# Storing the last gradient of wo in sixteen transfers of 15 down to 1 and 8 partitions in place of one

## The chip, the cores and the metric

The kernel runs on one core of a Trainium2 chip. The metric is the device time of one execution in microseconds (us). Each kernel is run several times, and the median is taken.

## The reference

The reference is one decode step of a transformer block with its backward pass. There is one token of 640 numbers, 32 heads of 128, and a cache of 8192 keys and values for each head. Everything is in bfloat16.

```
xn  = layernorm(x)
q   = xn @ wq                      # 640 x 4096, 32 heads of 128
p   = softmax(q . k_cache / sqrt(128))
att = (p . v_cache) @ wo           # wo is 4096 x 640
mlp = (silu(xn @ w1) * (xn @ w3)) @ w2
out = x + att + mlp
# the outputs: out, and the gradients of x, k_cache, v_cache, wq, wo, w1, w3, w2 for a given grad_out
```

The gradients of the caches are as large as the caches: 64 MB is read for each of K and V, and 64 MB is written for each gradient. The gradient of `wo` is an outer product: row n of it is `grad_out` times element n of the heads' outputs. It has 4096 rows of 640, and the kernel writes it in eight groups of four heads, 640 KB each.

## The kernel before, in words

The kernel begins with the feed-forward part (its products, its gradients of w1, w3 and w2), and then goes through the 32 heads. The loads of K and V for a head are 2 MB each and are issued by SyncE (SP). For each head VectorE multiplies K and V by the query and by the gradient row, TensorE sums the products, and VectorE and ScalarE form the two outer products that are the gradients of K and V, in tiles named `ot`. These are stored by GpSimd (POOL), 2 MB a tensor. In the last two heads (`TAIL = 2`) they are stored by SyncE instead, half a tensor (1 MB) at a time, at L456: eight such stores.

The order of instructions on every engine is written out by hand (`manual_schedule`). An engine works through its list in order. On SyncE, which has nothing but transfers, an issue that has to wait holds all issues behind it.

What comes after the loop is the tail. It finishes head 31, and then the following happens around the change:

- ScalarE forms the last quarter-group of the gradient of wq in `dwq_t` (L822) and issues its store of 640 KB itself (L824).
- VectorE forms the last group of the gradient of wo, in place in the tile `wo_g` (L826). SyncE stores it (L827), 128 partitions of four rows of 640, so 5120 bytes in a row of memory for each partition.
- VectorE and TensorE add up the remaining sums and finish the layernorm's backward pass (L832 to L853). Its result `dx_bf` is 1280 bytes, and SyncE stores it (L855).
- ScalarE stores the block's output `fin_bf`, five partitions of 256 bytes (L860).

Each transfer that SyncE or ScalarE issues counts up one of eight semaphores (`DMAHW0` to `DMAHW7`, numbers 100, 102, 103, 105, 106, 107, 109 and 110 in the trace) when its data has landed. The framework gives them out in turn, to both engines from one list, and a transfer that gets a semaphore waits at its issue until the transfer that had the semaphore before it has landed. In the kernel before, the eight stores of L456 have DMAHW4, 5, 6, 7, 0, 1, 2 and 3; then the store of `dwq_t` has DMAHW4, that of `fin_bf` DMAHW5, that of `wo_g` DMAHW6 and that of `dx_bf` DMAHW7. At the very end (L886) SyncE waits for all these semaphores, and the program ends.

Of the kernel before, what the change touches and what calls it, by code (L numbers as in the profile page):

```python
# [16 lines left out]
P = 128  # L17
# [4 lines left out]
def kernel(  # L22
# [22 lines left out]
    nc = tc.nc  # L45
# [23 lines left out]
    LANES = 16  # L69
# [26 lines left out]
    dwo_v = out_5.rearrange("(g p r) c -> g p r c", p=P, r=GH)  # L96
# [7 lines left out]
    with tc.manual_schedule(engines=ORDERED):  # L104
# [640 lines left out]
        for h in range(H - 1):  # L745
            n = new_head(h + 1) if h + 1 < H else None
            c = hs.pop(h)
            g, hh = divmod(h, GH)
# [50 lines left out]
        c = hs.pop(H - 1)  # L799
        g = c.g  # L800
# [23 lines left out]
        nc.scalar.dma_start(dwq_v[:, :, g * GH * DH:(g + 1) * GH * DH], dwq_t[:])  # L824
        for r in range(GH):
            nc.vector.tensor_scalar(c.G["wo"][:, r, :], g_bc_bf[:], on[:, r:r + 1], None, ALU.mult)  # L826
        nc.sync.dma_start(dwo_v[g], c.G["wo"][:])  # L827


        fin = consts.tile([P, NC], F32, name="fin")  # L830
# [3 lines left out]
        for ci in range(NC):  # L834
            k, c = divmod(ci * P, WIDE_COLS)
# [55 lines left out]
```

## Time and profile before

| what | value |
|---|---|
| median of 3 runs | 719.05 us (718.98 to 719.26) |
| the profiled execution, its time | 718.87 us |
| its span, first to last instruction | 717.1 us |
| PE, DVE, ACT busy | 78%, 88%, 68% of the span |
| moved | 303.32 MB, 423 GB/s in the mean |
| DMA issues of the tail | 1024 KB x8, 640 KB x2, 1.2 KB x2 |

The profiled execution lies 1.77 us above its span, and 0.18 us below the median of the runs. A page of the profile gives the busy time of each engine, the DMA share in forty slices, the chain of waits that ended last, groups of instructions with their mean duration, and the DMA issues with the time from issue to landing. "SPq" and "ACTq" are the sequencers of SyncE and ScalarE, which issue transfers. The chain of waits is followed back from the last instruction that computes; the stores that are still under way after it are not in it, and have to be read from the stretches of time after it and from the waits of SyncE.

### The profile page before, as it was taken

What the parts mean: (1) busy time and instruction counts of PE and PEld (TensorE: products, weight loads), DVE (VectorE), ACT (ScalarE), POOL (GpSimd) and SP (SyncE); (2) the same over time, 40 slices, a digit from 0 to 9 for tenths busy, and PEclk for the clock granted to TensorE, in tenths of its full rate; (3) what the DMA queues carried; (4) which work ended last, traced back from release to release, by engine and by line L of the source; (5) the groups of instructions that cost most, each with busy time, mean ns of one, the idle gap of its engine ahead of it and who ended that gap; (6) DMA issues with size and microseconds to landing.
All of it is one profiled execution on the core that took longest, in us unless ns stands there. A gap on an engine that the chain in (4) does not pass through costs nothing.

```text
span 717.1 us, 9854 instructions
## 1 busy us (share of the span) xinstructions
PE 557.1 (78%) x3516; PEld 272.4 (38%) x3516; DVE 630.6 (88%) x723; ACT 484.2 (68%) x1472; POOL 49.5 (7%) x91
## 2 busy tenths in 40 slices
PE   6878988878788777776887787488868789877772
PEld 4753443334333333333343344143434334333331
DVE  5789999999989895997899899499999889899982
ACT  1275778796769656694587867468677857777552
POOL 0010000000001110000000110000000000000100
PEclk9698999998989998997899989899999878999995
DMA  9999999999999999999999999999999999999997
GB/s 364 416 425 430 431 430 430 429 429 429 428 432 428 426 428 424 429 427 426 432 431 428 430 422 426 428 430 429 428 428 431 429 430 431 429 430 429 429 421 288
DMA packets 27039, 303.32 MB, mean 423 GB/s; under 512 B 3249, under 2 KB 3959, under 8 KB 9327
## 3 DMA queue, kind: packets, MB, share of 16 engines
q1 hardware_dynamic: 12832, 154.88, 50.9%
q0 software_dynamic: 10960, 137.72, 45.2%
q10 hardware_dynamic: 3198, 10.10, 3.5%
q8 instruction: 27, 0.44, 0.2%
q14 instruction: 22, 0.17, 0.1%
HBM read 151.34 MB, written 151.34 MB: 422 GB/s over the span
## 4 chain that ended last, share of the span: by engine, by line
DMA 45%; DVE 31%; PE 17%; ACT 3%; issue 2%; POOL 0%; ACTq 0%; DVEq 0%; POOLq 0%
DMA Kt<-in_A_k_cache_dram 28%; DVE T L425 15%; DMA out_dram<-ot 12%; DVE ot L451 10%; PE ob L500 4%; DMA lane_pad<-in_A_wq_dram 4%; PE psS L427 3%; PE psDP L427 3%; ACT ot L445 2%; DVE DP_sb L526 1%; DVE S_sb L472 1%; PE dh_ps L591 1%; PE dx_ps L626 1%; PE gate_ps L602 1%; PE ps_od L516 1%
## 5 line engine op out<-in xcount | busy, mean ns | idle before, releaser
L427 PE MATMUL psDP<-T,ident_bf 128*128 128x512 bf16 x512 | 157.0, 462 | 64.6 <-DVE T L425 64.6
L427 PEld LDWEIGHTS <-ident_bf 128*128 128x128 bf16 x1024 | 108.3, 109 | 212.6 <-issue 140.1
L445 ACT ACTIVATE ot<-qs_g,Uf 128x128 bf16<-128x128 bf16 x504 | 154.0, 394 | 45.1 <-DVE Uf L539 27.2
L425 DVE TENSOR_TENSOR T<-Kt,qs_g 128x4096 bf16<-128x4096 bf16 x64 | 146.4, 2287 | 20.0 <-DMA Kt<-in_A_k_cache_dram 18.8
L445 ACT ACTIVATE ot<-do_g,Pf 128x128 bf16<-128x128 bf16 x512 | 156.3, 389 | 6.2 <-DMA out_dram<-ot 5.2
L425 DVE TENSOR_TENSOR T<-Vt,do_g 128x4096 bf16<-128x4096 bf16 x64 | 146.0, 2282 | 3.9 <-DMA Vt<-in_A_v_cache_dram 3.9
L427 PE MATMUL psS<-T,ident_bf 128*128 128x512 bf16 x512 | 129.0, 397 | 17.7 <-DVE T L425 17.7
L451 DVE TENSOR_TENSOR ot<-qs_g,U 128x3072 bf16<-128x3072 bf16 (+2 forms) x64 | 112.6, 1760 | 11.9 <-DMA out_dram<-ot 11.8
L451 DVE TENSOR_TENSOR ot<-do_g,P 128x3072 bf16<-128x3072 bf16 (+2 forms) x64 | 112.3, 1755 | 6.3 <-DMA out_dram<-ot 5.2
L458 POOL DMA_DIRECT2D out_dram<-ot x60 | 32.2, 537 | 549.2 <-DVE Uf L539 303.6
L500 PE MATMUL ob<-Vt,P 128*4 128x512 bf16 x512 | 64.1, 394 | 0.0
L500 PE MATMUL ob<-Kt,U 128*4 128x512 bf16 x512 | 60.5, 379 | 1.4 <-DVE U L533 1.4
L494 ACT ACTIVATE Pf<-E,rZ 128x16 f32<-128x16 f32 (+1 forms) x32 | 9.8, 307 | 60.2 <-DVE rZ L489 60.2
L558 ACT ACTIVATE dq_diag<-ident_bf,odq 128x128 bf16<-128x128 bf16 x32 | 12.8, 401 | 47.8 <-DVE odq L554 47.8
L516 PEld LDWEIGHTS ps_od<-pick,wide 128*128 128x128 f32 x256 | 38.1, 213 | 7.8 <-issue 3.0
L516 PE MATMUL ps_od<-pick,wide 128*128 128x2 f32 x256 | 33.8, 254 | 0.5 <-ACT wide L508 0.5
L500 PEld LDWEIGHTS <-U 128*4 128x4 bf16 x512 | 19.8, 84 | 37.5 <-DVE U L533 6.6
L476 PE MATMUL sm<-ident_f,mrow 128*128 128x128 f32 x64 | 15.9, 331 | 22.3 <-DVE mrow L474 22.3
L500 PEld LDWEIGHTS <-P 128*4 128x4 bf16 x512 | 20.8, 86 | 25.8 <-issue 3.5
L508 ACT COPY wide<-ob 128x256 f32<-128x256 f32 x64 | 20.1, 363 | 12.7 <-PE ob L500 12.7
L472 DVE TENSOR_REDUCE S_sb<-psS 128x64 f32<-128x512 f32 x32 | 21.9, 685 | 5.6 <-PE psS L427 5.6
L317 ACT COPY woT<-ps_t 128x512 bf16<-128x512 bf16 x40 | 22.9, 577 | 4.2 <-PE ps_t L312 3.6
(174 smaller groups left out, 552.4 us busy)
## 6 DMA issues: line engine op xcount, KB each, us to landing
out_dram<-ot POOLq DMA_DIRECT2D x60, 2048.0 KB, 24.4
Kt<-in_A_k_cache_dram SPq DMA_DIRECT2D x32, 2048.0 KB, 26.6
Vt<-in_A_v_cache_dram SPq DMA_DIRECT2D x32, 2048.0 KB, 20.0
out_dram<-ot SPq DMA_DIRECT2D x8, 1024.0 KB, 12.7
out_dram<-wo_g ACTq DMA_DIRECT2D x6, 640.0 KB, 15.1
wo_g<-in_A_wo_dram ACTq DMA_DIRECT2D x6, 640.0 KB, 15.8
wq_two<-in_A_wq_dram SPq DMA_DIRECT2D x1, 2560.0 KB, 23.8
w1t<-in_B_w_dram SPq DMA_DIRECT2D x1, 2160.0 KB
```

What stands on the lines that cost most here:

```text
L317: nc.scalar.copy(woT[:], ps_t[:])
L425: nc.vector.tensor_tensor(T[:], src[:, :, ds_], vec[:, ds_].unsqueeze(1).to_broadcast([P, J, DHH]), ALU.mult)
L427: nc.tensor.matmul(ps[:], lhsT=ident_bf[:], rhs=T[:, :, RUN * i:RUN * (i + 1)], start=(half == 0 and i == 0), stop=(half == 1 and i == DHH ...
L445: nc.scalar.activation(st.ot[half][:, JH - n + j].rearrange("p a b -> p (a b)"), vec, ACTF.Copy, scale=wf[:, half, j:j + 1])
L451: nc.vector.tensor_tensor(st.ot[half][:, 0:n], vec.rearrange("p (a b) -> p a b", b=2).unsqueeze(1).to_broadcast([P, n, DH // 2, 2]), w2[:, ...
L458: nc.gpsimd.dma_start(dst.rearrange("p j d -> p (j d)"), st.rows[:])
L472: nc.vector.tensor_reduce(st.S[:], st.ps["S"][:], AX.X, ALU.add)
L476: nc.tensor.matmul(st.sm[:, 8:8 + P], lhsT=mrow[:].to_broadcast([P, P]), rhs=ident_f[:], start=True, stop=True, skip_group_check=True)
L500: nc.tensor.matmul(ob[c0:c0 + WIDE, :], lhsT=w2[:, WIDE * q:WIDE * (q + 1), 0], rhs=src[:, WIDE * q:WIDE * (q + 1), :].rearrange("p j d -> ...
L508: nc.scalar.copy(part[:], ob[:, i * (WIDE // 2) * DH:(i + 1) * (WIDE // 2) * DH])
L516: nc.tensor.matmul(st.od, lhsT=st.wide[i][:, b * DH:(b + 1) * DH], rhs=pick[:, r, :], start=(r == 0), stop=(r == WIDE - 1), skip_group_che ...
L558: nc.scalar.activation(dq_diag[:], ident_bf[:], ACTF.Copy, scale=odq[:, 1:2])
```

## The change

The one transfer of L827 becomes a loop of sixteen (L827 to L830 of the kernel after), all issued by SyncE, with the same bytes from the same tile. `LANES` is 16 and `P` is 128, so the counts of partitions are 15, 14, 13 and so on down to 1, which is 120 together, and then 8. Nothing else is changed; the later lines move down by three.

```diff
         for r in range(GH):
             nc.vector.tensor_scalar(c.G["wo"][:, r, :], g_bc_bf[:], on[:, r:r + 1], None, ALU.mult)
-        nc.sync.dma_start(dwo_v[g], c.G["wo"][:])
+        p0 = 0
+        for k in list(range(LANES - 1, 0, -1)) + [P - LANES * (LANES - 1) // 2]:
+            nc.sync.dma_start(dwo_v[g, p0:p0 + k], c.G["wo"][p0:p0 + k])
+            p0 += k
```

## The prediction

> **What bounds the kernel now.** I read the page first, then stretches of the tail, then SyncE's issues there, then its waits. The slices of the page:
>
> ```profile
> DMA  9999999999999999999999999999999999999997
> GB/s 364 416 425 430 431 430 430 429 429 429 428 432 428 426 428 424 429 427 426 432 431 428 430 422 426 428 430 429 428 428 431 429 430 431 429 430 429 429 421 288
> ```
>
> The DMA engines are full from first to last, so the kernel is bound by bytes until its last slice. There the stretches (busy time and count by engine, clock, DMA share, GB/s) show what is left:
>
> ```profile
> 700.00:708.00 8.00, 4.11 (x21) 3.08 (x21) 4.25 (x17) 3.13 (x6) 0.00 (x0) 0.61 1.01 419
> 708.00:712.00 4.00, 0.00 (x0) 0.00 (x0) 0.00 (x0) 0.00 (x0) 0.00 (x0) 0.50 0.76 285
> 712.00:714.00 2.00, 0.00 (x0) 0.00 (x0) 0.00 (x0) 0.00 (x0) 0.00 (x0) 0.50 0.38 137
> 714.00:715.00 1.00, 0.00 (x0) 0.00 (x0) 0.00 (x0) 0.00 (x0) 0.00 (x0) 0.50 0.10 34
> 715.00:717.10 2.10, 0.00 (x0) 0.00 (x0) 0.00 (x0) 0.00 (x0) 0.00 (x0) 0.50 0.00 1
> ```
>
> No engine computes after 708; stores alone set the end. The share falls in steps, so the sixteen DMA engines run dry one after the other, and at 0.10 one or two still work. Next the timeline of SyncE (start, length, issue), and the issues by tile (KB, us to landing):
>
> ```profile
> 702.11 0.41 SPq L827 DMA_DIRECT2D out_dram<-wo_g  x1
> 707.36 0.33 SPq L855 DMA_DIRECT2D out_dram<-dx_bf  x1
> ```
>
> ```profile
> out_dram<-ot SPq DMA_DIRECT2D x8, 1024.0 KB, 12.7
> out_dram<-wo_g SPq DMA_DIRECT2D x1, 640.0 KB, 13.4
> out_dram<-dwq_t ACTq DMA_DIRECT2D x1, 640.0 KB, 12.7
> out_dram<-dx_bf SPq DMA_DIRECT2D x1, 1.2 KB, 8.3
> ```
>
> Everything lands 8 to 13 us after its issue, because the queues are that long. Last, what SyncE waits for between 700 and 718:
>
> ```profile
> SPq L886 <- DMA out_dram<-ot: 5.2, 2, 2.8
> SPq L855 <- DVE fin_bf L859: 5.0, 1, 5.0
> SPq L886 <- DMA out_dram<-dwq_t: 2.7, 1, 2.7
> ```
>
> The end is a list of landings. The seventh store of L456 lands at 710.69 and the eighth at 713.17 (the two waits on `ot`, 5.2 us together), `dwq_t` at 715.87, and `fin_bf`, behind it on the same queue, at 716.06. From there to the span's end are 1.04 us of closing instructions.
>
> **The change: what it removes.** One issue of 0.41 us at 702.11. Nobody waited for it but the end, and it landed at 715.5, before `dwq_t`. Worth nothing by itself.
>
> **What it adds: waits.** No new bytes, and nothing on PE, DVE, ACT or POOL. But SyncE issues sixteen transfers, and there are eight completion semaphores. The list of the changed program, with the semaphores each issue waits for, reads:
>
> ```
> L829 DMACopy out_dram<-wo_g 15x2560 [waits DMAHW6_49,DVE_49]
> L829 DMACopy out_dram<-wo_g 14x2560 [waits DMAHW7_49]
> L829 DMACopy out_dram<-wo_g 13x2560 [waits DMAHW0_49]
> L829 DMACopy out_dram<-wo_g 12x2560 [waits DMAHW1_49]
> L829 DMACopy out_dram<-wo_g 11x2560 [waits DMAHW2_49]
> L829 DMACopy out_dram<-wo_g 10x2560 [waits DMAHW3_49]
> L829 DMACopy out_dram<-wo_g 9x2560 [waits DMAHW4_49]
> L829 DMACopy out_dram<-wo_g 8x2560 [waits DMAHW5_49]
> ...
> L858 DMACopy out_dram<-dx_bf 128x5 [waits DMAHW6_49,DVE_49]
> ```
>
> I call the parts 1 to 16. Each waits for the landing of the transfer that had its semaphore before, at these times in the trace of before. Parts 1 and 2: the third and fourth store of L456, long landed (695.7, 699.7). Part 3: the fifth store, 703.67. Part 4: the sixth, 707.36. Part 5: the seventh, 710.69. Part 6: the eighth, 713.17. Part 7: `dwq_t`, 715.87. Part 8: `fin_bf`, 716.06. Parts 9 to 16 wait for parts 1 to 8, and `dx_bf` for part 9. Queued behind part 7 on SyncE are nine parts and `dx_bf`, which was ready at 707.36; who waits for `dx_bf` is the end.
>
> **Part 7's wait.** `dwq_t` may land earlier than before, since fewer rows of `wo_g` share its DMA engines. In the packet records of the trace, a `wo_g` row of 5120 bytes takes 0.196 us and alternates with rows of `dwq_t` (0.046); each of the sixteen engines has eight `wo_g` rows. All eight gone would be 8 x 0.193 = 1.5 us sooner, none gone 0. By 713.2 six parts are issued, so up to six rows an engine are still in the way; on the last engine I count some 0.4 us gained. I take 715.45 for part 7's issue, between 714.4 and 715.9.
>
> **The issues after it.** From part 7's issue to that of `dx_bf` are ten periods. Lone issues take 0.22 us (one row, `g_row`), 0.30 (`fin_bf`, five rows) and 0.33 (128 rows), with 0.05 to the next. Parts 7 to 16 have 9 to 1 rows and then 8, nearest to `fin_bf`: 0.34 a period, 3.4 us. From below it is ten times 0.27; from above, the back-to-back issues of the kernel's start, 0.44 to 0.64, so 2.7 to 6.4. `dx_bf` is issued at 718.85. `fin_bf` lands before part 7's period is over and costs nothing; if it lands late, it costs what it is late. Part 15 needs part 7 landed, 2.7 us after its issue, which I take as just enough (below).
>
> **`dx_bf` and the end.** On engines that had run dry, `dx_bf` landed 1.5 to 1.8 us after its issue; on a busy one it took 8.3. By 718.85 nothing else is under way: 1.75, landing at 720.6. The closing 1.04 follow: span 721.65, against 717.1. With the 1.77 around the span this is 723.4 for the profiled execution, 4.5 above its 718.87, and the median of before was 719.05.
>
> [...]
>
> **Rivals.**
>
> *The waits don't hold, only the dealing counts.* If semaphores came free early, all parts would be issued by 708 and `dx_bf` at 707.8. The five packets of `fin_bf` sit on the five engines a small transfer uses, and those include the one that ends last (715.09) and the second last (714.50). If parts of k rows always go to the same first k engines, the first gets 16 rows, the fifth 12 and the last none, in place of 8 each: the late engine gets 4 to 8 rows more, 0.8 to 1.5 us, so 719.6 to 720.4. Against it: the waits stand in the program, and the final waits of before show the landings they wait for. 4%.
>
> [...]
>
> *Each part waits out the one eight before it.* If a part of few rows takes longer to land than the 2.7 us I leave, part 15 waits for 7, 16 for 8 and `dx_bf` for 9. At 4 us, say because the rows are still behind others, `dx_bf` is issued some 1.3 later: 724.7; at 5 us 725.7. For it: two of `fin_bf`'s five engines landed at 1.5 and 2.7 us, the others late behind `dwq_t`. Against it: the queues are empty by 716. 13%.
>
> *Issues cost as at the start.* At 0.44 to 0.64 a period the ten cost 1.0 to 3.0 more: 724.4 to 726.4. Against it: those are 64 or 128 rows each, here at most 9. 10%.
>
> *Faster.* The late engines lose up to eight rows of `wo_g` each, and `dwq_t` and `fin_bf` land up to 1.5 us sooner: 717.4. This decides only if `dx_bf` lands before 716.06, so is issued by 714.3, and part 7 by 710.9. `dwq_t` would have to land 5 us earlier, and the rows give 1.5 at most. 2%.
>
> **How the numbers follow.** The forecast case, 71%, ends between 714.4 + 2.7 + 1.5 + 1.0, a span of 719.6 (721.4 with the 1.77), and 715.9 + 4.4 + 2.0 + 1.04, one of 723.3 (725.1); all lows at once are unlikely, so I take 722.1 to 725.1 as its own range. With the rivals that make it later, the range is 722.1 to 725.8. About 0.2% of the time, 1.4 us, is what a measurement of this kernel can tell from no change. Forecast, long landings and slow issues are slower by more, 94%; the dealing lies at 0.1 to 0.2%, so 4% the same; 2% faster.
>
> **What would show it.** In the changed profile: parts 3 to 6 issued one by one at about 703.7, 707.4, 710.7 and 713.2; part 7 right after `dwq_t` lands, near 715.4; parts 8 to 16 back to back; `dx_bf` issued near 718.9 in place of 707.36, landing in under 2 us; the DMA share almost zero from 716 on, over a tail longer by some 4 us; nothing changed before 702. I am wrong if `dx_bf` is issued before 711, if `wo_g`'s parts are issued in one run from 702, or if a wait among parts 9 to 16 is longer than 0.5 us.

## The result, and the profile after

The changed kernel takes 724.79 us in the median of 4 runs (724.32 to 725.44), against 719.15 (718.98 to 719.71) for the kernel before beside it: a ratio of 1.0081 with a 95% interval of 1.0066 to 1.0096, some 5.6 us more. The forecast was 723.4 with a range of 722.1 to 725.8, slower. The profiled execution is the longest of the four, 725.44 us with a span of 723.6.

The slices of the page, DMA share and GB/s:

```profile
DMA  9999999999999999999999999999999999999994
GB/s 367 417 425 430 430 422 418 429 429 434 424 432 428 428 429 424 428 427 428 415 429 431 429 425 421 431 425 428 433 429 430 428 429 429 432 431 428 427 423 165
```

Only the last slice looks different at once: 165 GB/s against 288, in a slice of 18 us. The stretches of the tail (columns as in the prediction):

```profile
708.00:712.00 4.00, 0.58 (x3) 0.27 (x3) 1.03 (x5) 0.00 (x0) 0.00 (x0) 0.50 0.86 319
712.00:714.00 2.00, 0.00 (x0) 0.00 (x0) 0.00 (x0) 0.00 (x0) 0.00 (x0) 0.50 0.43 144
714.00:715.00 1.00, 0.00 (x0) 0.00 (x0) 0.00 (x0) 0.00 (x0) 0.00 (x0) 0.50 0.35 109
715.00:717.00 2.00, 0.00 (x0) 0.00 (x0) 0.00 (x0) 0.00 (x0) 0.00 (x0) 0.50 0.07 24
717.00:723.60 6.60, 0.00 (x0) 0.00 (x0) 0.00 (x0) 0.00 (x0) 0.00 (x0) 0.50 0.20 41
```

The DMA engines run almost dry by 717, as they did by 715 before, and then comes what was not there: 6.6 us at a fifth of their time. SyncE's timeline and its waits between 700 and 726 say what they do there:

```profile
702.92 0.33 SPq L456 DMA_DIRECT2D out_dram<-ot  x1
704.11 15.51 SPq L829 DMA_DIRECT2D out_dram<-wo_g  x16
719.71 0.36 SPq L858 DMA_DIRECT2D out_dram<-dx_bf  x1
```

```profile
SPq L829 <- DMA out_dram<-ot: 4.2, 3, 3.0
SPq L829 <- DMA out_dram<-dwq_t: 2.6, 1, 2.6
SPq L889 <- DMA out_dram<-wo_g: 1.2, 1, 1.2
SPq L889 <- DMA out_dram<-dx_bf: 0.9, 1, 0.9
```

The sixteen parts take SyncE 15.5 us. Within L829 it waits three times for stores of `ot` (parts 4, 5 and 6) and then 2.6 us for `dwq_t` (part 7); in the kernel before, waits of this kind stood at L886, where nothing was behind them. Part 3 did not wait: the store whose semaphore it has landed at 704.75, and SyncE was at the issue of part 2 until 705.69. The single issues are part 6 at 713.55, part 7 at 716.42, part 8 at 716.74, part 16 at 719.34. `dx_bf`, ready at 709.4 here, is issued at 719.71 and is the last to land, at 722.67.

### The profile page after: what moved, and what is told of

The parts are those of the page before. It is cut to its first block, busy times and chain, and to the rows that moved or that the text cites. A ratio compares the mean times of both kernels' runs of the same rounds, so it can differ in the third digit from the quotient of the medians.

```text
span 723.6 us, 9853 instructions
## 1 busy us (share of the span) xinstructions
PE 551.2 (76%) x3500; PEld 272.9 (38%) x3516; DVE 630.0 (87%) x723; ACT 484.4 (67%) x1472; POOL 49.5 (7%) x91
## 4 chain that ended last, share of the span: by engine, by line
DMA 45%; DVE 29%; PE 18%; ACT 2%; issue 2%; POOL 0%; ACTq 0%; DVEq 0%; POOLq 0%
DMA Kt<-in_A_k_cache_dram 32%; DVE T L425 14%; DMA out_dram<-ot 12%; DVE ot L451 9%; PE ob L500 4%; PE psS L427 4%; PE psDP L427 3%; ACT ot L445 2%; DVE DP_sb L526 1%; PE dx_ps L626 1%; PE dh_ps L591 1%; DVE S_sb L472 1%; PE gate_ps L602 1%; DMA g_row<-in_grad_out_dram 1%; PE ps_q L322 1%
## 5 line engine op out<-in xcount | busy, mean ns | idle before, releaser
L427 PE MATMUL psDP<-T,ident_bf 128*128 128x512 bf16 x512 | 152.5, 452 | 65.9 <-DVE T L425 65.9
L312 PE MATMUL ps_t<-ident_bf,wo_g 128*128 128x128 bf16 x160 | 16.1, 225 | 12.1 <-ACT dqbc_g L569 11.0
```

What stands on the lines that cost most here:

```text
L312: nc.tensor.transpose(ps_t[:, hh * DH:(hh + 1) * DH], wo_g[:, hh, ci * P:(ci + 1) * P], ident_bf[:])
L427: nc.tensor.matmul(ps[:], lhsT=ident_bf[:], rhs=T[:, :, RUN * i:RUN * (i + 1)], start=(half == 0 and i == 0), stop=(half == 1 and i == DHH ...
```

## The experiments

All are edits of the kernel before, unless the text says otherwise. `e` numbers give their order. For reading the profiles of several kernels together, times are often counted from the issue of the eighth store of L456; from there to the span's end it is 16.2 us in the kernel before and 20.7 in the changed one. The runs show that this issue itself moves by several us from one program to another, so the landings on each profile's own clock are given as well.

**e1, e2, e3: five, six and eight parts, each of 32 or 16 partitions.** Does the cost come in steps, where a wait begins to bind, or with each transfer?

```diff
-        nc.sync.dma_start(dwo_v[g], c.G["wo"][:])
+        p0 = 0
+        for k in [32, 32, 32, 16, 16]:      # e2: [32, 32, 16, 16, 16, 16]; e3: [16] * 8
+            nc.sync.dma_start(dwo_v[g, p0:p0 + k], c.G["wo"][p0:p0 + k])
+            p0 += k
```

> The store in five transfers of 32, 32, 32, 16 and 16 partitions, all dealt evenly. Theory (the waits on the eight semaphores): the fifth part waits for the seventh store of L456 (10 us after the eighth's issue), and dx_bf for the eighth store, 12.2 us after that store's issue, 713.2 on the clock of before. dx_bf then lands 1.8 to 3.0 us later, 715.0 to 716.2, as late as fin_bf does (716.06): 719.0 to 719.6, and 16.1 to 16.5 us from the eighth store's issue to the span's end, against 16.2 before and 20.7 with sixteen parts. Rival (each added transfer costs the same, 5.6 us over fifteen): four added ones cost 1.5, so 720.6. Rival (the program as such makes the loop before the tail longer): the eighth store is issued at 702 or later, against 700.9 before.

> The store in six transfers of 32, 32, 16, 16, 16 and 16 partitions. Theory: dx_bf now has the semaphore of dwq_t and waits until that lands, 715.3 to 715.9 on the clock of before; it lands 1.8 to 3.0 us later, and 0.95 follow: a span of 718.2 to 719.8, so 720.0 to 721.6, and 17.3 to 18.9 us from the eighth store's issue to the end. The step from five parts to six is 1 us or more. Rival (each added transfer costs the same): 721.0, but only 0.4 above five parts.

> The store in eight transfers of 16 partitions. Theory: the seventh part waits for dwq_t (715.0 to 715.9 on the clock of before), the eighth and dx_bf follow at 0.34 us each, dx_bf lands 1.8 to 3.0 us after its issue: a span of 718.4 to 720.5, so 720.2 to 722.3, some 0.5 above six parts. Rival (each added transfer costs the same): 721.8, 0.8 above six parts.

Measured: 720.80 us with five (ratio 1.0021, interval 1.0011 to 1.0030), 721.68 with six (1.0036, 1.0023 to 1.0049), 722.64 with eight (1.0058, 1.0036 to 1.0080), against 719.05. The waits of SyncE around the tail, with five and then with six:

```profile
SPq L829 <- DMA out_dram<-ot: 4.5, 2, 2.3
SPq L858 <- DMA out_dram<-ot: 2.5, 1, 2.5
```

```profile
SPq L858 <- DMA out_dram<-dwq_t: 2.6, 1, 2.6
SPq L889 <- DMA out_dram<-dx_bf: 1.9, 1, 1.9
```

The waits are where the theory put them. With five, `dx_bf` (L858) waits for the last store of `ot` and goes out 12.16 us after that store's issue; with six it waits for `dwq_t`, which lands 13.43 us after it, and goes out at 13.49, and the end then waits for `dx_bf` itself. With eight, part 7 goes out at 16.19, when `dwq_t` has landed at 16.18 (this profile is of the slowest of its four executions, 725.55 us; the others took 722.05 to 723.20). But the times do not decide between the theory and a cost per transfer. Five parts were to cost 0.5 us at most and cost 1.75: `dx_bf` landed 5.3 us after its issue, not 1.8 to 3.0, because the engines were still busy: `dwq_t` landed at 717.56 and part 5 at 717.74, where `dwq_t` landed at 715.87 before. The step from five to six is 0.9, between the 1 or more and the 0.4.

The count from the eighth store's issue to the end does not bear the theory out: 18.6 us with five parts, where 16.1 to 16.5 were expected, and 17.2 with six, where 17.3 to 18.9 were. That issue lies at 700.44 with five parts, but at 702.77 with six and 702.53 with eight, as the rival of a longer loop expected. By 700 us the DMA engines had moved 298.17 MB with six parts and 297.76 with eight, against 298.52 before, which is 0.8 and 1.8 us of their work at 428 GB/s. So in these two executions a part of the cost lies before the tail.

**e4: uneven dealing alone, in three transfers** of 49, 35 and 44 partitions in the same loop.

> The store in three transfers of 49, 35 and 44 partitions; no wait of these binds, and dx_bf is issued when it is ready. [...] The theory of the waits by itself expects no change from these three transfers but what the dealing does.

Measured: 721.16 us, ratio 1.0038 (1.0023 to 1.0052), 2.1 us more. In the semaphores' records the three transfers count up in 7, 7 and 11 steps beside the one that comes at once, which I read as so many engines at work (in the changed kernel a part of k rows counts up in k such steps, from 15 for part 1 to 1 for part 15). `dwq_t` lands on nine engines by 712.3 and on the other seven between 715.6 and 718.2; the five that `fin_bf` uses are among the seven. In equal shares, 49 = 7 x 7, 35 = 7 x 5 and 44 = 11 x 4, an engine that works for all three gets 7 + 5 + 4 = 16 rows in place of 8, and the late engines are seven. So it looks as if the rows of each transfer went to the same engines first; the trace has no numbers of engines that would show which. Not all of the 2.1 us need be the dealing: by 700 us the engines had moved 0.26 MB less than before, 0.6 us of their work. From the eighth store's issue, which came at 704.71 here, to the end it is 14.7 us, where it is 16.2 in the kernel before.

**e5: the kernel before, profiled a second time.**

> The kernel before, unchanged but for a comment, for a second profile of it: how far the place of the tail's landings differs between two executions of one program. If the profile of before is typical, the eighth store is issued at 700.4 to 701.4, dwq_t lands at 715.4 to 716.4 and the span is 716.9 to 718.4. If the engines' backlog at the end differs from execution to execution by 1 to 2 us, so do these.

Measured: 718.83 us, a span of 717.1. The eighth store is issued at 701.57, 0.65 later than in the first profile and just outside what was expected, and `dwq_t` lands at 715.84, against 715.87. So in these two executions the DMA engines' work ends at the same time, and the place of an issue in the tail differs.

**e6: two parts of 64 partitions.**

> The store in two transfers of 64 partitions, dealt evenly; dx_bf has the semaphore of the fifth store of L456, which lands before dx_bf is ready, so no wait binds. Theory (waits, and uneven dealing in the kernels that have it): no change, 718.9 to 719.5. Rival (each added transfer costs 0.37 us): 719.4. Rival (any splitting costs a step by itself, as five even parts suggest with 1.7): 720 or more.

Measured: 719.91 us against 718.82, ratio 1.0014 (1.0005 to 1.0024), its ten runs from 718.97 to 721.65. No wait binds, and the parts are equal (a load of 64 partitions, `dbc`, counts up in 16 steps in the kernel before), yet there is a cost of about 1 us. In the packet records a row of 5120 bytes of `wo_g` takes 202 ns in the mean in one transfer, 255 in two parts, 278 in five, 299 in six, 367 in eight parts of 16, and 298 in the sixteen of the change. Eight rows an engine at 255 in place of 202 are 0.4 us, at 298 0.8. So the rows of parts over fewer partitions took longer in the mean, which is a part of the cost that the prediction had left out. It is some of the rows: the median stays at 196 with two, five and six parts and is 336 with eight.

**e7 and e8: semaphores free.** The stores of head 30 and 31, of `dwq_t` and of `fin_bf` are moved to GpSimd (e7), and the sixteen parts are put into that (e8).

```diff
-    TAIL = 2
+    TAIL = 0
...
-        nc.scalar.dma_start(dwq_v[:, :, g * GH * DH:(g + 1) * GH * DH], dwq_t[:])
+        nc.gpsimd.dma_start(dwq_v[:, :, g * GH * DH:(g + 1) * GH * DH], dwq_t[:])
...
-        nc.scalar.dma_start(out_0.rearrange("a b (c p) -> (a b c) p", p=P), fin_bf[:])
+        nc.gpsimd.dma_start(out_0.rearrange("a b (c p) -> (a b c) p", p=P), fin_bf[:])
```

> A control for the next kernel: the eight stores of L456 go back to GpSimd as four of 2 MB, and dwq_t and fin_bf are stored by GpSimd too, so that SyncE's semaphores are all free when the last store of wo_g comes, in one transfer as before. I expect 719 to 722; its own number matters only as the base of the next.

> The control with the sixteen parts of 15 down to 1 and 8 on SyncE. The first eight find their semaphores free; parts 9 to 16 wait only for parts 1 to 8, which are not behind other stores on their queue. Theory (the cost is the wait for stores that land late): the parts are all issued within some 10 us of 702, dx_bf before 713, and the time is that of the control, or up to 1.5 us above it from the uneven dealing. Rival (sixteen transfers cost as such, 5.6 us): the control and 5 or more.

Measured: 723.84 us for the control (ratio to the kernel before 1.0072, 1.0057 to 1.0087) and 723.44 with sixteen parts (1.0064, 1.0047 to 1.0081). The control lies outside the 719 to 722 expected of it. By the times there is no cost, as the theory has it; but the profiles allow less than the times. The issues of L829 in e8 (shortest, median and longest in ns, first and last start):

```profile
L829 SPq DMA_DIRECT2D out_dram<-wo_g x16: 227/580/2082, 703.2 to 717.4; - x16
```

and what the end of the control waits for, by SyncE's waits and by GpSimd's instructions before the end:

```profile
SPq L886 <- DMA out_dram<-fin_bf: 8.4, 1, 8.4
L886 POOLq DRAIN  x3: 46/102/11966, 710.1 to 722.6; - x3
```

With no landing of another store to wait for, the sixteen issues still took 14.5 us, not some 10, because an issue right behind another on a loaded queue took up to 2.1 us. `dx_bf` went out at 717.79, where before 713 was expected, and landed at 720.76, the last of all. In the control the last landing is that of `fin_bf`, at 718.44, so sixteen parts end 2.3 us later. The time does not show it, because the control does not end with its landings: GpSimd's DRAIN, 12 us long, is over only at 722.09, 3.65 us after `fin_bf` has landed, and the program closes behind it. So this pair shows that sixteen transfers are free where something else ends last, not that they are free.

**e9 and e10: only `dwq_t` and `fin_bf` moved to GpSimd** (`TAIL` stays 2), with one transfer and with sixteen.

> A control: as the kernel before, but dwq_t and fin_bf are stored by GpSimd, so that they have semaphores of another set. One transfer of wo_g. The bytes and queues' load are the same; I expect 718.8 to 720.5.

> That control with the sixteen parts. Theory: no part waits for dwq_t or fin_bf any more; the longest wait is part 8's, for the eighth store of L456 (some 12.3 us after its issue, 713.2 to 714), then parts 9 to 16 and dx_bf follow at 0.33 us each (3.0), dx_bf lands 1.8 to 3.0 later and 0.95 follow: 721 to 723, that is 2 to 3.5 below the changed kernel's 724.8 and 1.5 to 3 above its control. Rival (sixteen transfers cost as such): 5.6 above the control, 724.5 or more.

Measured: the control 721.75 us (1.0038, 1.0024 to 1.0051), outside what I expected, and with sixteen parts 724.62 (1.0073, 1.0059 to 1.0087): 2.9 above its control, as the theory said, but outside the 721 to 723 that it gave, and only 0.2 below the changed kernel. In the waits of e10, `dwq_t` is gone from L829:

```profile
SPq L829 <- DMA out_dram<-wo_g: 1.7, 3, 0.7
SPq L829 <- DMA out_dram<-ot: 0.8, 1, 0.8
```

Part 8 goes out 11.92 us after the eighth store's issue, when that store has landed, and `dx_bf` at 16.41, against 16.79 in the changed kernel. So with the wait for `dwq_t` gone, `dx_bf` goes out only 0.4 us earlier: part 8's wait is 0.8 us, parts 9 to 11 wait for parts 1 to 3, and the issues before take 1.1 to 2.5 us each.

The profile also shows why the control is slower than the kernel before. Its last store lands at 716.64, where `fin_bf` landed at 716.05 before, but GpSimd's DRAIN holds the end. The kernel before, then the control:

```profile
L886 POOLq DRAIN  x3: 46/102/41395, 669.2 to 716.8; - x3
L886 POOLq DRAIN  x3: 46/106/9653, 710.1 to 720.3; - x3
```

The long one ends at 710.56 in the kernel before and at 719.76 in the control, 3.4 and 3.5 us after the last landing of a GpSimd transfer. In e10 `dx_bf` lands at 721.66, after that DRAIN, so the sixteen parts move the last landing by 5.0 us and the time by 2.9. By the landings this pair speaks as much for a cost of the transfers as such, which was to be 5.6, as for the wait.

**e11: the changed kernel, with `dx_bf` issued by ScalarE.**

```diff
-            nc.sync.dma_start(out_1.rearrange("a b (p c) -> p (a b c)", c=NC), dx_bf[:])
+            nc.scalar.dma_start(out_1.rearrange("a b (p c) -> p (a b c)", c=NC), dx_bf[:])
```

> The changed kernel, with dx_bf issued by ScalarE and so not behind the parts. Theory: the parts themselves still wait; part 6 now has the semaphore of dwq_t, part 16 is issued ten periods later and lands 2.4 us after that: 0.5 to 1.0 below the changed kernel, 723.8 to 724.4. Rival (only dx_bf's place behind the parts costs): back to 719 to 720.5.

Measured: 723.06 us, 1.7 below the changed kernel; ratio to the kernel before 1.0055 (1.0042 to 1.0069). More is gained than I expected, but nearly 4 us remain. `dx_bf` has long landed then, and the end is part 16, issued 15.63 us after the eighth store and landed at 17.57. So the parts hold the end by themselves, and `dx_bf` behind them adds its own slow landing.

**e12: one load of K in two halves, the tail as before.**

```diff
-            nc.sync.dma_start(Kt[:], kc[h])
+            for p0 in (0, P // 2) if h == 16 else (0,):
+                p1 = p0 + (P // 2 if h == 16 else P)
+                nc.sync.dma_start(Kt[p0:p1], kc[h, p0:p1])
```

> The kernel before, with one load of K in the middle (head 16) in two transfers of 64 partitions; its tail is as before. It asks where the 1 us of the two-part store comes from, of which the profile of its tail shows nothing. If it is the tail: no change here, 718.8 to 719.2, as narrow as before. If any change in the count of transfers moves the DMA engines' pace over the whole execution: 719.5 to 720.5, with a spread of 2 us.

Measured: 722.33 us, ratio 1.0048 (1.0035 to 1.0062): 3.2 us for one more transfer, far from the tail, and neither of the two expectations. The stretches show it to be local; the kernel before, then e12:

```profile
350.00:360.00 10.00, 8.96 (x65) 4.16 (x64) 9.93 (x9) 7.54 (x25) 0.53 (x1) 0.99 1.01 433
360.00:370.00 10.00, 7.97 (x52) 4.41 (x51) 9.79 (x13) 7.21 (x23) 0.53 (x1) 1.00 1.01 429
```

```profile
350.00:360.00 10.00, 8.72 (x61) 4.01 (x61) 9.90 (x12) 7.74 (x26) 0.53 (x1) 0.97 1.05 318
360.00:370.00 10.00, 7.46 (x46) 4.12 (x45) 7.90 (x9) 5.14 (x18) 0.53 (x1) 1.00 0.98 385
```

The engines are as busy as ever, but move 1.6 MB less in these 20 us, which is 3.7 us at 428 GB/s: the rows of 16 KB that take 612 ns before take 947 between 350 and 360. The slowing is of the kind seen in e6, with 2 MB in place of the 640 KB of `wo_g`. In both a row takes longer where a transfer covers fewer partitions (612 to 947 ns here with 64, 202 to 255 there with 64 and to 367 with 16). Why is not shown.

## Why the prediction was right, and where its sum was off

The direction, the place and the mechanism came as forecast: parts 4 to 6 are held by the stores of `ot` (part 3 was to be too, and was not), part 7 by `dwq_t`, parts 8 to 16 follow without a further wait, and `dx_bf`, ten periods later, is the last to land. That the wait for `dwq_t` ends last is shown by the changed kernel's waits, and by e2 and e3, where it moves to another instruction with the count of parts.

What that wait is worth is another question. From part 1's issue to that of `dx_bf` it is 15.60 us in the changed kernel, 15.22 in e10 without the wait for `dwq_t`, and 14.55 in e8 without any. So the waits decide when `dx_bf` goes out, but without them the issues on the loaded queue would have held it to within about 1 us of the same place. The prediction did not have this: it took all parts to be issued by 708 if the semaphores came free early.

The time falls into the range partly by luck. Part 7's issue and the landing of `dx_bf` lie beyond the bounds of their own terms (715.9 and 2.0), and the sum stays inside because the ten periods took 3.29 of the 4.4 us allowed. Two of the signs named did not come: the DMA share was not almost zero from 716 on (0.20 from 717), and something had changed before 702. The sum, term by term, on the clock of each profile:

| term | forecast | measured |
|---|---|---|
| part 7's issue | 715.45 | 716.42 |
| ten periods to `dx_bf` | 3.4 | 3.29 |
| `dx_bf` to its landing | 1.75 | 2.96 |
| closing | 1.04 | 0.98 |
| span | 721.65 | 723.65 |

**Part 7's wait** came 1.0 us later than I put it. `dwq_t` did land sooner after its issue, 11.2 us in place of 12.7, nearly the whole 1.5 that I had given as the bound. Not all of that is the rows that were out of its way: it was issued 2.0 us later while the engines were 1.3 us behind, which alone makes it 0.7 shorter and leaves some 0.8. And in this execution everything was later by then: the eighth store was issued 2.0 us later, and by 700 us the DMA engines had moved 297.97 MB against 298.52 before, 1.3 us of their work. The prediction had taken the time before 702 as unchanged, and that was wrong for this execution. The loss is in single stretches (0.26 MB between 100 and 120, 0.28 between 350 and 370). It is not a matter of the count of transfers: five parts had 298.55 MB by then, and e11, with the same sixteen, 298.61; eight parts had 297.76, and e9 with its one transfer 297.96. Its cause stays open. The profiled execution is also the longest of the four, by 0.65 over their median.

**The landing of `dx_bf`** was the term that I mis-sized: 2.96 in place of 1.75. The 2.0 with which it enters the upper end of the range is shown by no run: it took 2.96 us here and 2.61 in e2. The 1.5 to 1.8 us of the trace before were the first three of the sixteen counts of `dx_bf`'s semaphore, and the last one decides. e2 shows how long all sixteen take with nothing else under way: `dx_bf` is issued at 716.27, everything else has landed by 716.56, its packets run from 717.12 to 717.31, and its counts come from 717.58 to 718.88, 2.61 us after the issue. So most of the difference is the transfer's own. The rest fits with part 16, which goes out just before `dx_bf` in the changed kernel: four of its eight rows took 0.72 to 0.74 us in place of 0.196, and `dx_bf`'s last packet is over 1.26 us after the issue, against 1.04 in e2. In both kernels more than half of the landing lies between the last packet and the last count (1.70 and 1.57 us); why is not shown.

**The periods** were 0.33 us, as read from the issue of `fin_bf`.

**The rivals.** That only the dealing counts is refuted for this kernel, since the waits hold; but e4 fits its mechanism, at a cost of the size given (2.1 us, with 0.6 of it perhaps from before the tail, for 8 rows more, where 1.5 were worked out with rows of 0.193 us). That parts 9 to 16 wait for parts 1 to 8 did not happen in the changed kernel, and happened in e10 with three waits of 1.7 us together. That issues cost more was underrated: close behind another on a loaded queue they took 1.1, 1.6 and 1.4 us (parts 2 to 4), far above the 0.64 I took for the upper end. That end was read from the first 4 us of the trace; further on, at 6.02 and 11.20, two loads right behind others took 5.14 and 4.47 us to issue. In the changed kernel this was hidden, as part 6's wait ends later; in e8, where no wait hides it, it held `dx_bf` until 717.8. So taking away the waits alone would not have brought `dx_bf` back to 707.

**What the count of parts costs beside the waits** is settled only in part. Two parts cost 1.1 us with no wait at all. Five cost 1.75, and there even `dwq_t`, whose issue no part held, lands 1.7 us later than before. Slower rows give 0.4 and 0.6 of that as a mean over the engines, more on the one that ends last if it has the slow ones, and the rest is not explained.

## What to carry to other kernels

A transfer that nobody waits for can still hold the end once it is many transfers, because each needs one of the program's eight completion semaphores, and its issue waits for whoever had that semaphore before, in order, with everything behind it (6.8 us for parts 4 to 7 of the changed kernel). The issues alone can cost nearly as much where the queue is loaded (14.5 us for the sixteen in e8, without such waits, against 15.5), so taking the waits away need not give the time back. So for a split in a tail, list for each part whose landing it inherits, and see what is queued behind the first part that inherits a late one. Keep a store or load over all 128 partitions in one transfer: in the runs whose rows were read, from two parts (202 to 255 ns) to sixteen (298) and in e12 (612 to 947), they took longer in the mean. And before a kernel serves as a control, find what its end waits for: two controls here ended with GpSimd's DRAIN, 3.65 us (e7) and 3.1 us (e9) after their last store had landed.

## What the runs showed of the hardware that was not expected

- Rows of the same size took longer in the mean when a transfer covered fewer neighbouring partitions: 202 ns for 5120 bytes in a transfer of 128, 255 in two of 64 (e6), 367 in eight of 16 (e3); 612 ns for 16 KB, and 947 where a load was in halves of 64 (e12, between 350 and 360 us).
- An issue by SyncE right behind another, with the queue loaded, took 0.7 to 2.5 us (e8 and e10); after a pause of over 1 us, or with the queue empty, a part took 0.23 to 0.35 (in the changed kernel 0.25 to 0.30 for parts 6 to 16).
- GpSimd's long DRAIN before the end was over 3.4 to 3.65 us after the last landing of a transfer that GpSimd had issued, in all fourteen profiles. Where that did not hold the end, the span ended 0.97 to 1.16 us after the last landing.
- In e4 the transfer of 49 partitions counted up in 7 steps where one of 128 has 16, and `dwq_t` landed on nine engines by 712.3 and on the other seven from 715.6 on.
